# A spectral layer with two MLP layers on one core: weights converted in pairs of 512 columns, and what is done with fetched weights put at other places of a group

## The chip, the cores and the metric

The kernel runs on one core of one Trainium2 chip. The metric is the device time of one execution in microseconds. Five engines work side by side, each through its own instructions in order, and meet at semaphores: PE (TensorE, matmuls), DVE (VectorE), ACT (ScalarE), POOL (GpSimd) and SP (SyncE, which here issues nearly all DMAs). PEld is PE's loading of the stationary operand.

## The reference

Two batches of 3008 rows by 256 columns go through a spectral layer and then, as 6016 tokens, through two MLP layers. Cut to what matters:

```python
def _attn_ref(x, w_r, w_i, b_r, b_i):
    X = np.fft.rfft(x, axis=1)
    ...
    Yr = Xr @ w_r - Xi @ w_i + b_r
    Yi = Xr @ w_i + Xi @ w_r + b_i
    lam = 0.01
    Yr = np.sign(Yr) * np.maximum(np.abs(Yr) - lam, 0.0)
    ...
    y = np.fft.irfft(Y, n=x.shape[1], axis=1)

def _moe_ref(x, w_in, w_out):          # 256 -> 2048 -> 256
    h = x @ w_in
    g = h * (1.0 / (1.0 + np.exp(-1.702 * h)))
    return (g @ w_out).astype(np.float32)
```

The second MLP layer is the same with `np.exp(-h)`. The four weight matrices of the MLP layers arrive as 64-bit floats, bit for bit in integers, and are turned into 32-bit floats on the chip.

## The kernel before

**Stages.** The forward transform (`fwd`, 0 to 78 us), the complex product with threshold (`mid`, to 162), the inverse transform (`inv`, to 223), then the MLP (to about 1275). All matmuls take float32 numbers split into a high part `hi` and a low part `lo` and use three products, hi·hi, hi·lo and lo·hi.

**The MLP.** The tokens stand in six blocks, five of 1024 and a last one of 896. Each block runs through eight groups (p = 0 to 7), a group being 256 of the 2048 hidden columns; a group is written l.i.p here for layer l, block i and p. One group multiplies with seven combinations of the weight's and the input's quarters instead of eight (a scheme like Strassen's): 7 products of 3 matmuls, `prod` (L776), into banks X, Z, Y. ACT copies one product out (L798, L808, L810), DVE adds the next ones to it (L800, L817, L820), ACT applies the activation (L779) and casts its high part (L781), and POOL, for one of the four DVE, subtracts it for the low part (L786). The second matmuls (L748, 24 of them in a group, `out_next`) come a little later from a list. So a group has 21 + 24 = 45 matmuls; `hook(1)` to `hook(6)` are places in a group at which other work is written in. Ahead of each block the 7 combinations of its input are made (`xsums` L686 and L687 in group p = 6, `xprep` in p = 7 and in p = 0 of the new block: ACT casts L696, DVE subtractions L699 and L701).

**The weights.** A matrix is worked on in units of 128 of its 2048 columns or rows (256 numbers on each of 128 partitions), 64 units in all. `cv_load` fetches a raw unit of 256 KB (L146, on SP, two buffers). `cv_bits` converts it: ACT takes the absolute value scaled (L155), five DVE instructions shift and mask the bits (L160 to L164, queued in `fill` and emitted by `pump` or `fills`), and POOL adds the two parts (L223, in `settle`). Weights that are wanted soon are kept, the others spilled to DRAM (L226) and fetched later (L250, `cv_ld`). A first-layer weight, "in", that is kept or fetched gets four sums of its quarters (L195, L196, L198, L200), and the seven slots are cast (L99, ACT) and subtracted (L100) in `place_in`; an "out" weight only needs the cast and the subtraction, in `place_out`.

**What sets the order.** `tf`, `tm` and `ti` list the steps of the three transform stages at which a unit is converted (`tick`). `kb` and `kr` say how many units are converted in a group of block 0, and of blocks 1 to 4: 2 in each group of block 0 and 1 in each group after it. In the last block of layer 0 the weights of layer 1 are fetched, one "in" pair and one "out" pair for a group, and put at hooks 2 and 3 (`moved`). From group 0.0.1 on the program's order is each engine's order. In `fwd` POOL's and SP's order is the program's, in `mid` SP's and in `inv` PE's; there the rest is ordered by a list scheduler on a modelled timeline.

Of the kernel before, what the change touches and what calls it, by code (L numbers as in the profile page):

```python
# [10 lines left out]
CFG = {'lv0': 'V', 'lv': 'VVVVVPVVVVVP', 'dd0': 'VPVVPPPPPVVP', 'dd': 'VVVVVVVVVVPV', 'mpl': 'VPPVVP', 'ths': 'VVVVPV', 'thf': 'PVPVVPVV', 'fsl': 'VPVVVVPV', 'ivf': 'PVVPVVVVVPPVPPVV', 'cva': 'P', 'pol': 'PPPP', 'pil': 'P', 'mvl': 'PVVP', 'xl': 'V', 'xse': 'V', 'gl': 'VPPPPPPP', 'tf': [6, 9, 12], 'tm': [2, 3, 4, 5, 7, 14], 'ti': [2, 2, 3, 4, 5, 10, 12, 13, 13, 15], 'kb': [2, 2, 2, 2, 2, 2, 2, 2], 'kr': 1, 'fa': 3, 'fe': 2, 'xp': [2, 4, 4, 5], 'xq': [1, 4, 1], 'xs': 4, 'xi': [11, 12, 13, 15], 'xsi': 9, 'ca': 4, 'tl': True, 'fwd': 'Pool,SP', 'rest0': 'all', 'rest1': 'all', 'last1': 'all', 'inv': 'PE', 'mid': 'SP', 'last0': 'all', 'thm': 'A', 'gl0': 'PVPVVVPV', 'gl2': 'PPPPPPPP', 'gl3': 'PPPPPPPV', 'xl0': 'V', 'xl1': 'V', 'pre': 17, 'pre2': 0, 'yd': 6, 'nf': 4, 'lvb': 6, 'mlp': 'none', 'pr': 'VVVP', 'pf': 'PV', 'eo': '0000', 'ddb': 6, 'mlp1': 'all', 'mlp2': 'all'}  # L11
# [46 lines left out]
def spectral_mlp_kernel(ctx, tc, xin, m0, mfwd, minv, wc, bias, w_in1, w_out1, w_in2, w_out2, outT):  # L58
# [73 lines left out]
    pairs = [(kind, l, 2 * p, kept) for kind, l, p, kept in WEIGHTS]  # L132
    todo = [(kind, l, c + r, kept) for kind, l, c, kept in pairs for r in range(2)]
    loaded, bits, added, fill = [], [], [], []
    spilled, halves = {}, {}

    def cv_load(k=1):
        for _ in range(min(k, len(todo))):
            kind, l, c, kept = todo.pop(0)
# [33 lines left out]
    def place_out(l, c, a, lo_eng):  # L173
# [888 lines left out]
```

## Time and profile before

| | |
|---|---|
| runs timed | 1282.67, 1284.27, 1284.43 us; median 1284.27 |
| profiled execution | 1280.16 us, its span 1278.4 us |
| mean granted TensorE clock | 0.976 |
| PE busy | 1202.4 us, 94% |
| ACT / DVE / POOL busy | 801.0 / 751.9 / 587.3 us |
| DMA | 57.08 MB, mean 45 GB/s |

The profiled execution is one execution, 4.1 us below the median of the others; times within the trace are against its span. An engine's busy share is an average over stages in which it may be full or nearly idle. In a timeline, "[2.01 <-ACT yt L810]" means that the engine had been idle for 2.01 us and that the instruction of L810 on ACT released it.

### The profile page before, as it was taken

How to read it: one execution, taken by the hardware profiler on the slowest of the kernel's cores; microseconds unless marked ns; L12 is line 12 of the kernel's file. 1: busy time of each engine (PE TensorE's matmuls, PEld its weight loads, DVE VectorE, ACT ScalarE, POOL GpSimd, SP SyncE). 2: the span in 40 equal slices, each digit the busy share in tenths (PEclk: the TensorE clock that was granted, in tenths of full speed). 3: DMA queues.
4: the chain of work that ended last, by engine and by line, in shares of the span. 5: the costliest groups of instructions: out<-in, count | busy, mean ns of one | idle time of the engine just before them, and what ended most of it. 6: DMA issues, size and time to landing. Idle time of an engine off the chain costs nothing.

```text
span 1278.4 us, 15403 instructions
## 1 busy us (share of the span) xinstructions
PE 1202.4 (94%) x5220; PEld 973.4 (76%) x5220; DVE 751.9 (59%) x1222; ACT 801.0 (63%) x1585; POOL 587.3 (46%) x516
## 2 busy tenths in 40 slices
PE   7889869699899999999999879999999999999998
PEld 4867669477688787787887767887888888888897
DVE  7889999777756756657655564243352442623522
ACT  3556544566666667666666667666575665765764
POOL 4667665585444444444443434434333333333343
PEclk9999889989899999999999998999999999999999
DMA  8442114011111111111110110000000000000000
GB/s 321 165 156 62 42 46 154 25 45 46 37 39 37 37 38 34 41 38 33 38 38 9 34 40 27 1 1 34 1 33 1 1 34 1 1 34 1 34 1 29
DMA packets 33009, 57.08 MB, mean 45 GB/s; under 512 B 3233, under 2 KB 22689, under 8 KB 31650
## 3 DMA queue, kind: packets, MB, share of 16 engines
q1 hardware_dynamic: 30882, 41.42, 10.2%
q0 software_dynamic: 2048, 14.68, 3.1%
q8 instruction: 41, 0.67, 0.2%
q14 instruction: 38, 0.31, 0.1%
HBM read 44.68 MB, written 11.40 MB: 44 GB/s over the span
## 4 chain that ended last, share of the span: by engine, by line
PE 55%; ACT 9%; DVE 7%; issue 3%; DVEq 0%; ACTq 0%
PE o L748 29%; PE x L776 26%; ACT yt L779 3%; ACT g L781 2%; DVE yt L817 1%; DVE x L699 1%; ACT yt L798 1%; ACT x L696 1%; DVE yt L800 1%; DVE wi L100 1%; ACT yt L808 0%; DVE cv_c L160 0%; DVE cv_a L162 0%; ACT wi L99 0%; ACT yt L810 0%
## 5 line engine op out<-in xcount | busy, mean ns | idle before, releaser
L786 POOL TENSOR_TENSOR g<-yt,g 128x512 fp32r<-128x512 f32 (+1 forms) x288 | 372.5, 1305 | 567.7 <-DVE g L786 301.2
L748 PE MATMUL o<-g,wo 128*128 128x512 f32 (+1 forms) x2304 | 580.6, 394 | 3.2 <-ACT g L781 1.2
L776 PE MATMUL x<-x,wi 128*128 128x512 f32 (+1 forms) x2016 | 518.6, 396 | 36.6 <-ACT yt L810 15.6
L748 PEld LDWEIGHTS o<-g,wo 128*128 128x128 f32 x2304 | 437.5, 190 | 101.0 <-POOL g L786 1.8
L776 PEld LDWEIGHTS x<-x,wi 128*128 128x128 f32 x2016 | 379.0, 190 | 133.6 <-ACT yt L810 21.7
L779 ACT ACTIVATE yt<-yt 128x512 f32<-128x512 f32 (+1 forms) x288 | 179.0, 622 | 295.2 <-DVE yt L817 248.3
L781 ACT CAST g<-yt 128x512 fp32r<-128x512 f32 (+1 forms) x384 | 234.1, 611 | 11.7
L817 DVE TENSOR_TENSOR yt<-yt,x 128x512 f32<-128x512 f32 (+1 forms) x96 | 64.8, 675 | 210.4 <-PE x L776 210.2
L800 DVE TENSOR_TENSOR yt<-yt,x 128x512 f32<-128x512 f32 (+1 forms) x96 | 64.9, 676 | 174.5 <-ACT yt L798 173.5
L786 DVE TENSOR_TENSOR g<-yt,g 128x512 fp32r<-128x512 f32 (+1 forms) x96 | 66.1, 688 | 66.5 <-ACT g L781 66.4
L699 DVE TENSOR_TENSOR x<-yt,x 128x512 fp32r<-128x512 f32 (+1 forms) x48 | 54.3, 1132 | 28.7 <-ACT x L696 28.7
L223 POOL TENSOR_TENSOR cv_a<-cv_a,cv_c 128x256 f32<-128x256 f32 x64 | 62.9, 988 | 15.7 <-DVE cv_c L164 15.6
L820 DVE TENSOR_TENSOR yt<-yt,x 128x512 f32<-128x512 f32 (+1 forms) x96 | 64.9, 676 | 2.2 <-PE x L776 1.1
L779 ACT ACTIVATE yt<-x 128x512 f32<-128x512 f32 (+1 forms) x96 | 56.2, 585 | 3.9 <-PE x L776 3.9
L810 ACT COPY yt<-x 128x512 f32<-128x512 f32 (+1 forms) x96 | 55.7, 580 | 1.0 <-PE x L776 1.0
L798 ACT COPY yt<-x 128x512 f32<-128x512 f32 (+1 forms) x96 | 54.8, 571 | 1.8 <-PE x L776 1.8
L808 ACT COPY yt<-x 128x512 f32<-128x512 f32 (+1 forms) x96 | 54.9, 571 | 0.0
L358 PE MATMUL psi<-m,fh 128*128 128x376 f32 (+3 forms) x208 | 48.9, 324 | 3.0 <-ACT fh L99 1.7
L498 PE MATMUL psm<-wc_hi,xtl 128*128 128x512 f32 x96 | 40.0, 419 | 4.7 <-DVE xtl L100 3.8
L163 DVE TENSOR_SCALAR cv_c<-cv_a 128x256 uint32<-128x256 uint32 x64 | 43.3, 678 | 1.4
L155 ACT ACTIVATE cv_c<-raw 128x256 f32<-128x256 f32 x64 | 27.4, 438 | 22.9 <-DMA raw<-in_wi 19.8
L358 PE MATMUL psf<-m,xh 128*128 128x376 f32 (+1 forms) x160 | 37.1, 330 | 4.6 <-ACT xh L305 3.6
(109 smaller groups left out, 1140.9 us busy)
## 6 DMA issues: line engine op xcount, KB each, us to landing
raw<-in_wi SPq DMA_DIRECT2D x32, 256.0 KB, 2.7
raw<-in_wo SPq DMA_DIRECT2D x32, 256.0 KB, 2.6
raw<-in_x SPq DMA_DIRECT2D x12, 512.0 KB, 4.8
out_t<-yt SPq DMA_DIRECT2D x20, 256.0 KB, 2.0
m<-in_mf POOLq DMA_DIRECT2D x4, 1128.0 KB, 7.7
m<-in_mi POOLq DMA_DIRECT2D x4, 1128.0 KB, 7.5
w_out<-cv_a SPq DMA_DIRECT2D x24, 128.0 KB, 1.7
cv_ld<-w_out SPq DMA_DIRECT2D x24, 128.0 KB, 2.0
```

The source lines that it names most:

```text
L223: E('cva', u[2]).tensor_add(a, a, c)
L358: nc.tensor.matmul(ps, a, z, start=i == 0 and x == 0, stop=i == last and x == 2)
L699: E('xl1' if l else 'xl0' if i == 0 else 'xl', k).tensor_sub(lo, src, r32(hi))
L748: nc.tensor.matmul(acc[h, mm], st, mv, start=first and k == 0, stop=last and k == 2)
L776: nc.tensor.matmul(ps, st, mv, start=first and m == 0, stop=m == 2, skip_group_check=True)
L779: nc.scalar.activation(g, g if src is None else src, func)
L781: nc.scalar.copy(gh, g)
L786: eng.tensor_sub(gl, g, r32(gh))
L798: nc.scalar.copy(y1, X)
L800: nc.vector.tensor_add(y1, y1, Y)
L817: nc.vector.tensor_add(y2, y2, X)
L820: nc.vector.tensor_add(y3, y3, Z)
```

## The change

A unit becomes a pair: 256 columns or rows, 512 numbers on each partition, 32 pairs. The raw buffer holds a pair (an "in" pair comes by two DMAs, an "out" pair by one) and there is one such buffer in place of two. Each of the conversion's instructions, the POOL addition and the spill is 512 wide and there are half as many. The lists become `tm` [2, 4, 7], `ti` [2, 5, 13] (they were [2, 3, 4, 5, 7, 14] and [2, 2, 3, 4, 5, 10, 12, 13, 13, 15]; `tf` stays [6, 9, 12]), `kb` [1, 1, 1, 1, 1, 1, 1, 0] and `kr` [0, 1, 0, 1, 0, 1, 1, 0]: in the last group of every block and in groups 0, 2 and 4 of blocks 1 to 4 nothing is converted. The core of the rest:

```diff
+            raw = cv_p.tile([P, 2 * CU], mybir.dt.int64, tag="raw", name="raw64", bufs=1)
             if kind == "in":
+                r = raw[:, :].rearrange("p (s f) -> p s f", s=4)
+                src = w[:, 2 * p * P : 2 * (p + 1) * P].rearrange("(k p) f -> p k f", p=P)
+                nc.sync.dma_start(out=r[:, 1:3], in_=src[:, :, :P])
+                nc.sync.dma_start(out=r[:, 0:4:3], in_=src[:, :, P:])
...
-        c = cv_p.tile([P, CU], F32, tag="c", name="cv_c", bufs=4)
-        a = cv_p.tile([P, CU], F32, tag="a", name="cv_a", bufs=N("ca"))
+        c = cv_p.tile([P, 2 * CU], F32, tag="c", name="cv_c", bufs=2)
+        a = cv_p.tile([P, 2 * CU], F32, tag="a", name="cv_a")
...
-        fill.extend(
-            (
-                lambda: add(t12[:, 0], a1[:, 0], a1[:, 1]),
-                lambda: sub(t34[:, 0], a0[:, 0], a1[:, 0]),
-                lambda: put(slice(0, 2), a0),
-                lambda: sub(t12[:, 1], t12[:, 0], a0[:, 0]),
-                lambda: put(2, a1[:, 1]),
-                lambda: sub(t34[:, 1], a0[:, 1], t12[:, 1]),
-                lambda: put(slice(3, 5), t12),
-                lambda: (put(slice(5, 7), t34), w_in.update({(l, p): w})),
-            )
+        return (
+            lambda: add(t[:, 0], a[:, 0], a[:, 3]),
+            lambda: sub(t[:, 2], a[:, 1], a[:, 0]),
+            lambda: sub(t[:, 1], t[:, 0], a[:, 1]),
+            lambda: sub(t[:, 3], a[:, 2], t[:, 1]),
+        ), (
+            lambda: put(slice(0, 3), a[:, 1:4]),
+            lambda: (put(slice(3, 7), t), w_in.update({(l, p): w})),
         )
...
-        fills(1 if l or i == last else 2)
+        fills(1)
...
-    def moved(fetched):
-        for (kind, l, c), tiles in fetched:
-            for r, a in enumerate(tiles):
-                if kind == "in":
-                    place_in(l, c + r, a, nc.vector, sums_c)
-                else:
-                    place_out(l, c + r, a, nc.gpsimd)
+    def moved(h):
+
+        for (kind, l, p), a in fetched:
+            if kind == "in" and h == 2:
+                sums, puts[:] = place_in(l, p, a, nc.gpsimd, sums_c)
+                for f in sums:
+                    f()
+            if kind == "out" and h == 3:
+                place_out(l, p, a, nc.gpsimd)
+        if h == 3:
+            while puts:
+                puts.pop(0)()
...
-                cv_load(2 - len(loaded) if rate(at + 1) else 0)
+                cv_load(1 - len(loaded))
```

So of a fetched "in" weight the four sums are emitted at hook 2, the casts at hook 3, which stands behind the copies L808 and L810, and its low parts move from DVE to POOL. A kept or fetched "in" weight is put with two casts of 384 and 512 columns in place of four. In the whole program DVE has 1032 instructions where it had 1224, ACT 1507 where it had 1587, POOL 473 where it had 521 and SP 133 where it had 189; PE has the same number. Lines behind the conversion stand 3 lines earlier in the changed kernel.

**ACT, a group in the middle of the last block of layer 0** (`wi` and `wo` are the placed weights, `cv_ld` what was fetched, `cv_s` the sums, `g` the high part of an activation, `yt` the token buffer). Before:

```order
L781 CAST g<-yt 128x448
L99 CAST wi_6516<-cv_ld 128x256
L99 CAST wi_6516<-cv_ld 128x128
L99 CAST wi_6516<-cv_s 128x256 x2
L808 COPY yt<-x 128x448
L810 COPY yt<-x 128x448
L99 CAST wo<-cv_ld 128x256 x2
L779 ACTIVATE yt<-yt 128x448
```

And of the changed kernel:

```order
L778 CAST g<-yt 128x448
L805 COPY yt<-x 128x448
L807 COPY yt<-x 128x448
L99 CAST wo<-cv_ld 128x512
L99 CAST wi_6066<-cv_ld 128x384
L99 CAST wi_6066<-cv_s 128x512
L776 ACTIVATE yt<-yt 128x448
```

The two copies stand ahead of every cast of a weight now; before, four casts, two of them of the sums, stood ahead of them.

**DVE, group p = 0 of a new block (1 to 2)** (`x` after `<-` in L817 is a product on PE, `x<-yt,x` in L699 a low part of the block's input). Before:

```order
L800 TENSOR_TENSOR yt<-yt,x 128x512
L699 TENSOR_TENSOR x<-yt,x 128x512 x2
L160 TENSOR_SCALAR cv_c<-cv_c 128x256
L161 TENSOR_SCALAR cv_c<-cv_c 128x256
L162 SCALAR_TENSOR_TENSOR cv_a<-raw_3898,cv_c 128x256
L699 TENSOR_TENSOR x<-tmp,x 128x512
L163 TENSOR_SCALAR cv_c<-cv_a 128x256
L164 SCALAR_TENSOR_TENSOR cv_c<-raw_3898,cv_c 128x256
L752 COPY yt<-o_3428 128x512
L817 TENSOR_TENSOR yt<-yt,x 128x512
```

And of the changed kernel:

```order
L797 TENSOR_TENSOR yt<-yt,x 128x512
L696 TENSOR_TENSOR x<-yt,x 128x512 x2
L696 TENSOR_TENSOR x<-tmp,x 128x512
L749 COPY yt<-o_3156 128x512
L814 TENSOR_TENSOR yt<-yt,x 128x512
```

The five instructions of a conversion that stood between the additions L800 and L817 are gone from this group; so they are in group p = 7 before it.

**SP, at the change from kept to spilled weights, in block 1** (`raw` is the raw buffer, `w_in_0` the place of a spill). Before:

```order
L146 DMA raw_3140<-in_wi 128x2x128
L146 DMA raw_3142<-in_wi 128x2x128
L146 DMA raw_3258<-in_wi 128x2x128
L146 DMA raw_3260<-in_wi 128x2x128
L226 DMA w_in_0_3277<-cv_a 128x256
L226 DMA w_in_1_3280<-cv_a 128x256
L146 DMA raw_3367<-in_wi 128x2x128
L226 DMA w_in_2_3386<-cv_a 128x256
L146 DMA raw_3460<-in_wi 128x2x128
```

And of the changed kernel:

```order
L145 DMA raw_2911<-in_wi 128x2x128
L146 DMA raw_2911<-in_wi 128x2x128
L145 DMA raw_3188<-in_wi 128x2x128
L146 DMA raw_3188<-in_wi 128x2x128
L223 DMA w_in_0_3206<-cv_a 128x512
L145 DMA raw_3350<-in_wi 128x2x128
L146 DMA raw_3350<-in_wi 128x2x128
L223 DMA w_in_1_3368<-cv_a 128x512
```

Each raw tile is now written by two DMAs, into the one buffer that the conversion before it has read, and the spills are half as many and twice as large.

## Rows read from the trace of the kernel before

**Rows 1.** The windows view: from and to (us) and length, then busy time of PE, PEld, DVE, ACT and POOL with their instructions, the granted clock, the DMA share and GB/s. The row is `mid` and `inv` together.

```profile
78.00:223.00 145.00, 130.52 (x612) 107.77 (x612) 143.38 (x242) 79.12 (x155) 94.27 (x84) 0.93 0.24 81
```

**Rows 2.** Groups of DVE's instructions by line and shape in 78 to 223 us: busy time, mean ns of one, idle time before them. They are the conversion.

```profile
L164 DVE SCALAR_TENSOR_TENSOR cv_c<-raw,cv_c 128x256 f32<-128x256 uint32 x15 | 9.9, 668 | 0.0
L162 DVE SCALAR_TENSOR_TENSOR cv_a<-raw,cv_c 128x256 uint32<-128x256 uint32 x15 | 9.8, 661 | 0.0
...
L161 DVE TENSOR_SCALAR cv_c<-cv_c 128x256 uint32<-128x256 uint32 x15 | 7.8, 525 | 0.1
L160 DVE TENSOR_SCALAR cv_c<-cv_c 128x256 f32<-128x256 f32 x15 | 7.4, 502 | 0.5 <-ACT cv_c L155 0.5
L163 DVE TENSOR_SCALAR cv_c<-cv_a 128x256 uint32<-128x256 uint32 x15 | 6.5, 436 | 0.0
```

**Rows 3.** The same view of DVE in the forward transform, 0 to 78 us: two lines of the conversion, and L336, a tensor_scalar 512 wide.

```profile
L164 DVE SCALAR_TENSOR_TENSOR cv_c<-raw,cv_c 128x256 f32<-128x256 uint32 x5 | 2.1, 412 | 0.0
...
L161 DVE TENSOR_SCALAR cv_c<-cv_c 128x256 uint32<-128x256 uint32 x5 | 1.3, 277 | 0.0
...
L336 DVE TENSOR_SCALAR wc_lo<-wc_lo 128x512 fp32r<-128x512 f32 x1 | 0.4, 407 | 0.0
```

**Rows 4.** The same view of POOL, first in 78 to 223 us, then of the whole span.

```profile
L223 POOL TENSOR_TENSOR cv_a<-cv_a,cv_c 128x256 f32<-128x256 f32 x15 | 18.9, 1262 | 15.6 <-DVE cv_c L164 15.6
...
L786 POOL TENSOR_TENSOR g<-yt,g 128x512 fp32r<-128x512 f32 x240 | 316.4, 1330 | 487.2 <-DVE g L786 296.4 <-PE x L776 67.8 <-DVE yt L752 48.0
```

**Rows 5.** PE's timeline (start, duration, operation, how many in a row, wait ahead): the first row of 12 output matmuls in groups of block 0 and at its end, and after them the waits view of 223 to 350 us (total, times, longest).

```profile
255.04 6.03 PE L748 MATMUL o<-g,wo 128*128 128x512 f32 x12 [1.17 <-ACT g L781]
...
319.95 2.96 PE L748 MATMUL o<-g,wo 128*128 128x512 f32 x12
...
348.41 2.96 PE L748 MATMUL o<-g,wo 128*128 128x512 f32 x12
...
PE x L776 <- DVE yt L817: 10.5, 6, 3.4
```

**Rows 6.** PE's timeline at the border of blocks 1 and 2 of layer 0, and (last two rows) in layer 1 from group p = 7 of block 0 to the start of block 2, nine groups.

```profile
411.41 2.96 PE L748 MATMUL o<-g,wo 128*128 128x512 f32 x12
...
429.44 2.33 PE L776 MATMUL x<-x,wi 128*128 128x512 f32 x9 [1.17 <-DVE yt L817]
...
434.77 2.96 PE L748 MATMUL o<-g,wo 128*128 128x512 f32 x12
...
861.29 2.96 PE L748 MATMUL o<-g,wo 128*128 128x512 f32 x12
...
956.63 2.96 PE L748 MATMUL o<-g,wo 128*128 128x512 f32 x12
```

**Rows 7.** PE's timeline in the last block of layer 0 and, last two rows, of layer 1; the sixth row is the waits view of 692 to 800 us.

```profile
695.89 1.50 PE L776 MATMUL x<-x,wi 128*128 128x448 f32 x6 [2.01 <-ACT yt L810]
...
702.77 2.62 PE L748 MATMUL o<-g,wo 128*128 128x448 f32 x12
...
757.11 2.63 PE L748 MATMUL o<-g,wo 128*128 128x448 f32 x12
...
763.35 2.61 PE L776 MATMUL x<-x,wi 128*128 128x448 f32 x6 [3.61 <-ACT yt L810]
...
787.79 2.96 PE L748 MATMUL o<-g,wo 128*128 128x512 f32 x12
...
PE x L776 <- ACT yt L810: 15.6, 8, 3.6
...
1208.40 2.63 PE L748 MATMUL o<-g,wo 128*128 128x448 f32 x12
...
1217.64 2.63 PE L748 MATMUL o<-g,wo 128*128 128x448 f32 x12
```

**Rows 8.** The timeline of all engines inside group 0.5.3 of that block.

```profile
714.24 1.23 DVE L100 TENSOR_TENSOR wi<-cv_ld,wi 128x256 fp32r<-128x256 f32 x1 [0.91 <-ACT wi L99]
715.39 0.28 DVE L198 TENSOR_TENSOR cv_s<-cv_s,cv_ld 128x128 f32<-128x128 f32 x1
...
715.70 0.81 ACT L99 CAST wi<-cv_s 128x256 fp32r<-128x256 f32 x2 [1.30 <-DVE cv_s L198]
...
717.43 1.50 PE L776 MATMUL x<-x,wi 128*128 128x448 f32 x6 [1.27 <-ACT yt L810]
```

**Rows 9.** The timelines of DVE and (third row) POOL in group p = 6 of a block in which both `xsums` and a conversion stand, and of DVE in an ordinary group.

```profile
485.40 0.69 DVE L800 TENSOR_TENSOR yt<-yt,x 128x512 f32<-128x512 f32 x1 [2.06 <-ACT yt L798]
...
488.04 1.38 DVE L160 TENSOR_SCALAR cv_c<-cv_c 128x256 f32<-128x256 f32 x1
...
487.55 1.73 POOL L786 TENSOR_TENSOR g<-yt,g 128x512 fp32r<-128x512 f32 x1
...
491.04 0.69 DVE L817 TENSOR_TENSOR yt<-yt,x 128x512 f32<-128x512 f32 x1
...
459.54 0.69 DVE L817 TENSOR_TENSOR yt<-yt,x 128x512 f32<-128x512 f32 x1 [1.50 <-PE x L776]
```

**Rows 10.** DMA issues of the page (KB each, us to landing), and the waits view of ACT over the span.

```profile
raw<-in_wi SPq DMA_DIRECT2D x32, 256.0 KB, 2.7
...
raw<-in_x SPq DMA_DIRECT2D x12, 512.0 KB, 4.8
...
ACT cv_c L155 <- DMA raw<-in_wi: 19.8, 7, 5.2
```

More of the change, by code (lines that the diff above doesn't have):

```diff
@@ L234, in window @@
             if u[0] == "in":
-                place_in(u[1], u[2], a, E('pil', u[2]), sums_tmp)
+                for part in place_in(u[1], u[2], a, E('pil', u[2]), sums_tmp):
+                    fill.extend(part)
             else:
@@ L244, in tick, with fetch @@
         pump()
-        cv_load(2 - len(loaded))
-    def fetch(kind, l, c):
-        tag, n = ("a", 4) if kind == "in" else ("ld", 2)
-        a = cv_p.tile([P, CU], F32, tag=tag, name="cv_ld", bufs=n)
-        nc.sync.dma_start(out=a, in_=spilled[kind, l, c])
+        cv_load(1 - len(loaded))
+    def fetch(kind, l, p):
+        a = cv_p.tile([P, 2 * CU], F32, tag="a" if kind == "in" else "ld", name="cv_ld", bufs=2 if kind == "in" else 1)
+        nc.sync.dma_start(out=a, in_=spilled[kind, l, p])
         return a
@@ L837, in spectral_mlp_kernel @@
     for c in range(0, NFC // 2, 2):
-        moves.setdefault((0, 0, c // 2), []).append(("out", 0, c))
+        moves.setdefault((0, 0, c // 2), []).append(("out", 0, c // 2))
     for p in range(NPR):
-        moves.setdefault((0, last, p + 1) if p < NPR - 1 else (1, 0, 0), []).append(("in", 1, 2 * p))
-        moves.setdefault((0, last, p + 3) if p < NPR - 3 else (1, 0, p - NPR + 3), []).append(("out", 1, 2 * p))
-    def moved(fetched):
-        for (kind, l, c), tiles in fetched:
-            for r, a in enumerate(tiles):
-                if kind == "in":
-                    place_in(l, c + r, a, nc.vector, sums_c)
-                else:
-                    place_out(l, c + r, a, nc.gpsimd)
+        moves.setdefault((0, last, p + 1) if p < NPR - 1 else (1, 0, 0), []).append(("in", 1, p))
+        moves.setdefault((0, last, p + 3) if p < NPR - 3 else (1, 0, p - NPR + 3), []).append(("out", 1, p))
+    def moved(h):
[9 more added lines that the diff above has]
+                puts.pop(0)()
+    puts = []
     def rate(at):
@@ L854, in rate @@
         l, i, p = seq[at]
-        return 0 if l == 1 or i == last else N('kb')[p] if i == 0 else N('kr')
+        return 0 if l == 1 or i == last else N('kb' if i == 0 else 'kr')[p]
     def fetch_for(at):
-        units = moves.get(seq[at], ()) if at < len(seq) else ()
-        return [(u, [fetch(u[0], u[1], u[2] + r) for r in range(2)]) for u in units]
+        return [(u, fetch(*u)) for u in (moves.get(seq[at], ()) if at < len(seq) else ())]
     fetched = fetch_for(0)
@@ L886, in hook @@
                 xsums(*nxt)
-            if h == (3 if len(done) < 3 else 1):
+            if h == (3 if len(done) < 2 else 1):
                 window(0, done)
@@ L892, in hook @@
             if h in (2, 3):
-                moved([f for f in fetched if (f[0][0] == "in") == (h == 2)])
+                moved(h)
             if h == 5:
```

44 lines of the change are left out of this document (19 added, 25 removed).

## The prediction

> **What bounds the kernel now.** I read the windows view first, to see which engine is full in which stage; then PE's timeline, to see where the spacing of equal groups differs; then the waits of those places, and the timeline of all engines inside one such group.
>
> Three kinds of place come out. Ahead of the MLP, in `mid` and `inv`, DVE is busy for 143.38 of 145 us, while PE works for 130.52 [rows 1]: what DVE does there sets the pace. In most of the MLP PE is full: in layer 1 nine groups from 861.29 to 956.63 take 95.34 us, 10.5 each and 0.84 over [rows 6]. There nothing but fewer matmuls would help, and the change leaves PE's instructions alone. Between these lie the places with a spacing above 10.5 us (9.24 for 448 columns, 1217.64 − 1208.40 [rows 7]): block 0, the borders of blocks in layer 0, and its last block. There PE waits for an addition on DVE (L817) or a copy on ACT (L810), because those stand in order behind weight conversion or weight placing. So the question is how much of this excess goes, place by place.
>
> **The change part by part.** The sum is made against the profiled execution, 1280.16 us, and then set against the median of the runs, 1284.27.
>
> *Conversion ahead of the MLP.* 15 units are converted in 78 to 223 us and cost DVE 9.9 + 9.8 + 7.8 + 7.4 + 6.5 = 41.4 us, 2.76 each [rows 2]. Undisturbed, in the forward transform, the two kinds take 412 and 277 ns [rows 3], so a unit is 2 × 0.41 + 3 × 0.28 = 1.66; the other 1.10 is what POOL beside it and the crowd cost. A pair of 512 columns undisturbed is 3 × 0.41 (L336, [rows 3]) + 2 × 0.69 (the 512-wide L817, [rows 9]) = 2.6. If the disturbance stays 1.10 for a chain of five instructions, a pair costs 3.7, and 7.5 pairs cost 28: 14 us saved. If it doubles with the width, 4.8 and 36: 5 us saved. Part of what DVE saves will not reach the end, since PE has only 14.5 us of idle time in this stretch [rows 1]. Against it stands one raw buffer in place of two: a pair can be fetched only when L164 of the pair before has read it. ACT already waits 19.8 us in seven waits for raw units of 256 KB that land 2.7 us after issue; 512 KB of `in_x` took 4.8 [rows 10]. The list spreads pairs over steps of about 7 us, so most of this is covered by the transforms' other work; if two pairs in `inv`, where ACT also does the copies, were caught in full, it would cost 2 × 4.8 − 5 ≈ 4. I take 7, between −4 and 14, nearer the dear pair because POOL's additions get wider too (L223 alone has a mean of 1.26 us at 256 columns, [rows 4]).
>
> *Conversion in block 0.* From 255.04 to 319.95 five groups take 64.91 us, 12.4 over 52.5; six waits for L817 make 10.5 us of waiting in the block [rows 5]. Two units a group, ten DVE instructions, become one pair, five instructions: 3.3 undisturbed becomes 2.6, and where POOL's wide subtractions alternate with them, five places for it instead of ten. That is 0.7 to 2 us for each of seven groups, in 4 or 5 of which the wait ends last. I take 5. The bound above is 10 (nearly all of the waits); below, −1: `fills(1)` now puts the whole chain at one place, and wide instructions hold L817 up for longer when it is ready in their midst.
>
> *The border of blocks 0 and 1.* Two groups from 319.95 to 348.41 take 28.46, 7.5 over 21 [rows 5]. Layer 1 has the same border without conversion, at 0.84 over [rows 6]. As groups p = 7 and p = 0 have no conversion now, up to 6.6 goes. What is late next is the input's combinations (L699), whose chain is as long in both layers; after a stall the first matmuls also ran slowly: 12 in 6.03 us at 255.04 where 2.96 is usual [rows 5, 6], TensorE's lower clock. I take 5.5 (3 to 6.6).
>
> *The borders 1 to 2, 2 to 3 and 3 to 4.* The first takes 434.77 − 411.41 = 23.36 us for two groups, 2.36 over, 1.17 of it waiting for L817 [rows 6]; the same in layer 1 is inside the stretch that has only 0.84 over in nine. Three borders are 7.1. But group p = 6 of blocks 1 to 4 keeps a conversion beside `xsums`. There L800 ends at 486.1, the sums and a 256-wide chain follow, and L817 starts at 491.04 without having waited for PE: no slack at all, with L160 drawn out to 1.38 us beside a POOL subtraction of 1.73 [rows 9]. A 512-wide chain is 2.6 − 1.66 = 0.9 longer, so PE waits some 0.8 in four such groups, 3.2. In an ordinary group L817 still waits 1.50 for PE [rows 9], which covers the 0.9. Net 4 (2 to 6).
>
> *The last block of layer 0, its middle.* In a group the casts of the sums (ACT, 715.70) wait 1.30 us for L198, which stands behind L100, itself drawn out to 1.23 us; the copies L808 and L810 come behind those casts, and PE waits 1.27 us for L810 [rows 8]. Five groups from 702.77 to 757.11 take 54.34, 8.1 over 46.2, and the group before waits 2.01 at 695.89 [rows 7]. With the casts behind both copies, ACT has nothing in front of them that waits for a sum. The sums stay on DVE, without the low parts: fewer instructions ahead of L817. What is late next is POOL: it gets low parts of 384, 512 and 512 columns, at 1.33 for 512 [rows 4] about 3.7 us, between its subtractions of `g`. Its three subtractions of `g` take at most 3 × 1.33 = 4.0, together 7.7 of a group's 9.24, so I expect them to fit, if tightly. I take all of it, 10 (8 to 10.1).
>
> *Its last group and the first of layer 1.* From 757.11 to 787.79 two groups take 30.68; 9.24 + 10.5, and half a us because products are already 512 wide, leave 10.5 over, with a wait of 3.6 at 763.35 [rows 7]. Here `xprep` and the placing meet in one group; the placing still has to be done (the first group of layer 1 wants its weight), so I take 7 (4 to 10).
>
> Fewer DMAs on SP and 80 fewer instructions on ACT I cost at nothing: PE's work in the MLP hides both; uncovered, ACT's 48 casts saved would be at most a gain inside the last two terms.
>
> The sum: 7 + 5 + 5.5 + 4 + 10 + 7 = 38.5. That makes 1241.7 of the profiled execution, and 1245.8 of the median, for which I say 1246.
>
> **The rivals.**
>
> *A. POOL and DVE hold each other up as long as before.* L160 took 1.38 us beside a POOL instruction that took 1.73, where 0.28 and 1.33 are usual [rows 3, 4, 9]; so both are stretched by overlap, and a wider instruction may simply be stretched for longer. Against it: a chain has half as many places at which this can happen. Then the first two terms are nothing and the stall of group 6 doubles (four times 1.6 leave 0.7 of that term): 5.5 + 0.7 + 10 + 7 = 23, 1261 us. The Trainium skill, "SBUF — State Buffer", section "Who interferes with whom", says this outright: a DVE instruction with two SBUF inputs contends with GpSimd's reads, and whoever holds the shared port pair in DVE's two-port modes keeps it for the whole instruction while the other stands still. The stretched rows agree; that the loss grows with the width no row here shows. By that rule the sum would be 23, without it 38.5.
>
> *B. The stall moves to POOL.* Low parts of fetched weights now queue ahead of those of `g`, and output matmuls wait for them. For it: three of a group's four low parts of `g` are POOL's, and a low part of 512 takes as long as one of `g` [rows 4]; against it, the 1.5 us that are left of a group. If 1 us in each of the eight groups comes back, 8.5 of the last two terms' 17 go: 1254.
>
> *C. The clock comes along.* In 78 to 223 us the granted clock is 0.93 [rows 1], so 0.07 × 145 = 10 us hang on it. If a steadier stream there lets TensorE stay at the upper of its levels, up to that is added: 1236.
>
> *D, slower: the single raw buffer.* A fetch starts only after the pair before has been read, ACT's L155 waits for it, and ACT's copies and casts for PE queue behind L155. If all nine pairs ahead of the MLP pay 4.8 us [rows 10] on the path, that is 43 in place of a gain of 7; with the other 31.5 the change loses 11.5: 1296. It decides from 31.5 / 9 = 3.5 us a pair. Against it: DVE, not the fetch, ended nearly everything there, and the ticks lie far apart.
>
> *E. It comes to nothing.* A and B together with a small loss ahead of the MLP: 1284.
>
> The Trainium skill, "Perfetto Trace Analysis", section "Optimizing Scalar/DVE Operations", says that larger instructions help where the engine is saturated, and that smaller ones may finish a needed result sooner where it isn't but causes bubbles elsewhere. Rows 1 put `mid` and `inv` in the first case; rows 9 put group 6 in the second. By the second half, group 6 gets worse, as in my fourth term; by the first alone that term would be 7.1 and the sum 41.6.
>
> **How the numbers follow.** The forecast 0.52, A 0.17, B 0.10, C 0.13, D 0.05, E 0.03. The likeliest one's own range, from the bounds of its terms taken together, is 1236 to 1256. To hold eight in ten it has to reach A above and C below: 1229 to 1265. A measurement of this kernel can tell about 0.2%, 2.6 us, from no change. A, B, C and the forecast are all faster by more: 0.92. Within that: E, 0.03. Slower: D, 0.05.
>
> **What would show it.** In the profile of the changed kernel: groups of the last block at 9.24 us and no wait for the second copy (L807 there); the border of blocks 0 and 1 at 22 to 24 us for two groups instead of 28.46, later borders at 21; a wait of about 0.8 for L814 in group 6 of blocks 1 to 4; the five lines of a pair at 3.7 to 4.8 us ahead of the MLP, and the start of the MLP some 7 us earlier than 223. A shows as POOL's and DVE's 512-wide means far above 1.33 and 0.69 and an unmoved start; B as waits of output matmuls for POOL in the last block; D as long waits of L155 for `raw`. I am wrong if the start of the MLP moves back, or if most of the excess of the last block is still there.

## The result and the profile after

Three runs of the changed kernel took 1249.27, 1249.22 and 1248.68 us, median 1249.22, against 1284.27 before: a ratio of 0.9729, 95% interval 0.9707 to 0.9752. The forecast was 1246, so 35.05 us of the 38.5 came. The profiled execution took 1249.27 us, with a span of 1247.4; against the profiled execution of before that is 31.0 us, and the other 4.1 are what that one execution lay below its own median.

From the page of the changed kernel, its engines (busy, share, instructions) and one line of its groups:

```profile
PE 1190.4 (95%) x5220; PEld 967.2 (78%) x5220; DVE 708.4 (57%) x1030; ACT 790.1 (63%) x1505; POOL 593.3 (48%) x468
...
L773 PE MATMUL x<-x,wi 128*128 128x512 f32 (+1 forms) x2016 | 513.5, 393 | 20.9 <-ACT yt L807 8.6
```

PE's idle time ahead of its product matmuls fell from 36.6 us to 20.9, and its busy time by 12.0 us for the same 5220 matmuls; where that comes from follows with the table below. POOL is busier by 6 us with fewer instructions: they are wider, and it has the low parts that DVE gave up.

The windows view of the stretch ahead of the MLP, which answers to [rows 1], and DVE's lines in it, which answer to [rows 2]; L534 is work that has nothing to do with the weights:

```profile
78.00:221.00 143.00, 130.12 (x609) 107.78 (x609) 137.97 (x201) 74.80 (x136) 87.18 (x71) 0.93 0.24 81
...
L534 DVE TENSOR_TENSOR f<-th 128x256 f32<-128x256 f32 x28 | 22.8, 857 | 0.2
...
L165 DVE SCALAR_TENSOR_TENSOR cv_a<-raw,cv_c 128x512 uint32<-128x512 uint32 x7 | 7.2, 1025 | 0.0
L167 DVE SCALAR_TENSOR_TENSOR cv_c<-raw,cv_c 128x512 f32<-128x512 uint32 x7 | 6.8, 965 | 0.1
...
L166 DVE TENSOR_SCALAR cv_c<-cv_a 128x512 uint32<-128x512 uint32 x7 | 4.8, 682 | 0.0
L164 DVE TENSOR_SCALAR cv_c<-cv_c 128x512 uint32<-128x512 uint32 x7 | 4.7, 677 | 0.1
...
L163 DVE TENSOR_SCALAR cv_c<-cv_c 128x512 f32<-128x512 f32 x7 | 2.9, 414 | 0.1
```

The chain is now 7.2 + 6.8 + 4.8 + 4.7 + 2.9 = 26.4 us for seven pairs, 3.77 each, where 15 units took 41.4. DVE's busy time fell by 5.4 us only, in a stretch 2 us shorter. In the same view of before L534's line reads:

```profile
L537 DVE TENSOR_TENSOR f<-th 128x256 f32<-128x256 f32 x28 | 16.1, 619 | 0.1
```

These 28 subtractions and additions, the same in both kernels, take 6.7 us more.

PE's timeline from the MLP's start on, first matmuls of a product and the rows of 12 output matmuls that answer to [rows 5 to 7]:

```profile
221.39 2.95 PE L773 MATMUL x<-x,wi 128*128 128x512 f32 x12
...
246.18 2.93 PE L773 MATMUL x<-x,wi 128*128 128x512 f32 x6 [6.09 <-ACT yt L807]
...
266.06 2.96 PE L745 MATMUL o<-g,wo 128*128 128x512 f32 x12
...
316.59 2.96 PE L745 MATMUL o<-g,wo 128*128 128x512 f32 x12
...
337.63 2.97 PE L745 MATMUL o<-g,wo 128*128 128x512 f32 x12
...
676.59 2.63 PE L745 MATMUL o<-g,wo 128*128 128x448 f32 x12
685.83 2.63 PE L745 MATMUL o<-g,wo 128*128 128x448 f32 x12
...
732.25 2.63 PE L745 MATMUL o<-g,wo 128*128 128x448 f32 x12
...
756.86 2.96 PE L745 MATMUL o<-g,wo 128*128 128x512 f32 x12
```

Each of these stands at the same place of the program as a row of before: 316.59 as 319.95, 337.63 as 348.41, 685.83 as 702.77, 732.25 as 757.11, 756.86 as 787.79; 676.59 as 691.26, 266.06 as 268.66 and 221.39 as 223.13, three more rows of before's timeline. The lengths between them give the account:

| stretch | before | after | gained | forecast |
|---|---|---|---|---|
| up to the MLP's start | 223.13 | 221.39 | 1.7 | 7 |
| block 0, to its last group | 96.82 | 95.20 | 1.6 | 5 |
| border of blocks 0 and 1 | 28.46 | 21.04 | 7.4 | 5.5 |
| from there to the last block, with three borders and the group ahead of the fourth | 342.85 | 338.96 | 3.9 | 4 |
| last block, six groups | 65.85 | 55.66 | 10.2 | 10 |
| its last group and the first of layer 1 | 30.68 | 24.61 | 6.1 | 7 |
| all | | | 30.9 | 38.5 |

The last four came as forecast within 2 us, the first two at a third and less. In block 0, 6.09 us of waiting in one group stay, for a copy on ACT, and 5.9 in four waits for L814; the kernel before waited 8.8 us there in four waits for L817, and never for L810.

Part of two lines of the table is the clock. The windows view of the border of blocks 0 and 1 and of the last line's two groups, before and then after:

```profile
319.95:348.41 28.46, 24.96 (x91) 18.62 (x90) 20.94 (x35) 18.05 (x36) 13.05 (x14) 0.88 0.13 37
757.11:787.79 30.68, 23.94 (x91) 19.87 (x90) 18.46 (x34) 22.19 (x45) 10.81 (x11) 0.83 0.09 26
```

```profile
316.59:337.63 21.04, 21.04 (x91) 16.81 (x90) 14.22 (x19) 15.95 (x31) 10.38 (x8) 1.00 0.00 1
732.25:756.86 24.61, 21.16 (x92) 16.42 (x91) 18.42 (x27) 20.21 (x38) 16.29 (x13) 1.00 0.11 33
```

With the stalls gone TensorE was granted its upper level all the way, 1.00 where the mean was 0.88 and 0.83, and PE was busy for 3.9 and 2.8 us less with the same matmuls. So 3.9 of the 7.4 us and 2.8 of the 6.1 are faster matmuls, the rest shorter waits.

### The profile page after: what moved, and what is told of

Read it like the earlier page. It is cut to its first block, busy times and chain, and to the rows that moved or that the text cites. A ratio compares the mean times of both kernels' runs of the same rounds, so it can differ in the third digit from the quotient of the medians.

```text
span 1247.4 us, 14957 instructions
## 1 busy us (share of the span) xinstructions
PE 1190.4 (95%) x5220; PEld 967.2 (78%) x5220; DVE 708.4 (57%) x1030; ACT 790.1 (63%) x1505; POOL 593.3 (48%) x468
## 4 chain that ended last, share of the span: by engine, by line
PE 68%; DVE 15%; ACT 8%; issue 5%; POOL 3%; DMA 1%; SPq 0%; DVEq 0%; POOLq 0%; ACTq 0%
PE o L745 35%; PE x L773 31%; ACT yt L776 2%; ACT g L778 2%; DVE f L534 1%; PE psf L352 1%; DVE fl L100 1%; DVE cv_a L165 1%; DVE cv_c L166 1%; DVE th L518 1%; DVE yt L665 1%; DVE cv_c L163 1%; ACT x L693 1%; DVE yt L797 1%; DVE yt L814 1%
## 5 line engine op out<-in xcount | busy, mean ns | idle before, releaser
L783 POOL TENSOR_TENSOR g<-yt,g 128x512 fp32r<-128x512 f32 (+1 forms) x288 | 377.2, 1322 | 535.7 <-DVE g L783 275.2
L745 PE MATMUL o<-g,wo 128*128 128x512 f32 (+1 forms) x2304 | 574.3, 391 | 1.8 <-POOL g L783 1.2
L773 PE MATMUL x<-x,wi 128*128 128x512 f32 (+1 forms) x2016 | 513.5, 393 | 20.9 <-ACT yt L807 8.6
L745 PEld LDWEIGHTS o<-g,wo 128*128 128x128 f32 x2304 | 433.1, 188 | 97.6 <-POOL g L783 2.3
L814 DVE TENSOR_TENSOR yt<-yt,x 128x512 f32<-128x512 f32 (+1 forms) x96 | 64.8, 675 | 230.6 <-PE x L773 230.5
L817 DVE TENSOR_TENSOR yt<-yt,x 128x512 f32<-128x512 f32 (+1 forms) x96 | 64.8, 675 | 0.7
L696 DVE TENSOR_TENSOR x<-yt,x 128x512 fp32r<-128x512 f32 (+1 forms) x48 | 49.8, 1038 | 25.6 <-ACT x L693 25.6
L795 ACT COPY yt<-x 128x512 f32<-128x512 f32 (+1 forms) x96 | 54.8, 571 | 5.3 <-PE x L773 3.7
L220 POOL TENSOR_TENSOR cv_a<-cv_a,cv_c 128x512 f32<-128x512 f32 x32 | 48.7, 1523 | 12.9 <-DVE cv_c L167 12.2
L495 PE MATMUL psm<-wc_hi,xth 128*128 128x512 f32 x96 | 40.5, 422 | 4.4 <-ACT xth L99 4.4
L355 PEld LDWEIGHTS psi<-m,fh 128*128 128x128 f32 x208 | 38.1, 201 | 6.6 <-DVE sd L508 4.6
L495 PE MATMUL psm<-wc_hi,xtl 128*128 128x512 f32 x96 | 38.5, 406 | 1.6 <-DVE xtl L100 1.6
L355 PE MATMUL psi<-m,fl 128*128 128x376 f32 (+3 forms) x104 | 34.8, 334 | 5.4 <-DVE fl L100 3.0
```

The source lines that it names most:

```text
L355: nc.tensor.matmul(ps, a, z, start=i == 0 and x == 0, stop=i == last and x == 2)
L495: nc.tensor.matmul(t, a, w, start=(n == 0), stop=(n == 11 and grp == 1))
L745: nc.tensor.matmul(acc[h, mm], st, mv, start=first and k == 0, stop=last and k == 2)
L773: nc.tensor.matmul(ps, st, mv, start=first and m == 0, stop=m == 2, skip_group_check=True)
L783: eng.tensor_sub(gl, g, r32(gh))
L814: nc.vector.tensor_add(y2, y2, X)
```

## The experiments

All start from the changed kernel unless it is said otherwise; the ratios are against the kernel before on the same chip. Where an edit adds lines, lines behind it stand 2 to 5 later.

**The kernel before once more.**

> The kernel before as it is, for a second profile: the first one's execution was 4.1 us below the median. If a stage varies between executions, the MLP's start (223.1 us there) moves by some us in this one, while the groups from 0.1.2 on keep their lengths to 0.05 us; if nothing varies, 1280 us and 223 again.

1283.62 us. The first matmul of the MLP in it, by PE's timeline:

```profile
225.73 1.55 PE L776 MATMUL x<-x,wi 128*128 128x512 f32 x6
```

That is 2.6 us later than in the first profile, while from group 0.1.2 to the middle of the last block each group is as long as there to 0.05 us. So the stretch ahead of the MLP varies from execution to execution. The changed kernel and eight of the kernels below have the same work in the same order ahead of the MLP on PE, DVE, ACT and POOL; theirs starts at 219.4 to 222.4, 220.7 in the mean. Against 224.4, the mean of before's two, the first line of the table is rather 3.7 than 1.7. Much of the spread is made in the forward transform: the first product of `mid` stands at 76.4 to 79.1 us, and from there to the MLP's start the nine take 143.0 to 144.3, before's two 144.9 and 147.4.

**The chain in halves.**

```diff
-                lambda: ts(c, c, C_HI, None, op0=ALU.min),
+        for h in range(2):
+            v = slice(h * CU, (h + 1) * CU)
...
+                    lambda v=v: ts(c[:, v], c[:, v], C_HI, None, op0=ALU.min),
...
```

> Each of the five DVE instructions of a pair's conversion is split into two of 256 columns; all else is the changed kernel (loads, buffers, tables, places). Theory (what a pair costs on DVE is per instruction, disturbance by POOL included): a pair ahead of the MLP costs 2 x 2.76 = 5.5 us instead of 3.77, seven pairs 12 us more of DVE time, of which the MLP's start shows a part (2 to 6 us later than 221.4) and block 0 another 2 to 4; 1252 to 1258 us. Rival (the width of the instructions is nothing, the gain came from where things stand): within 2 us of 1249.

1263.62 us (four runs, 1262.67 to 1265.19; ratio 0.9847, 0.9832 to 0.9862). More than the theory's range: of the 14.4 us the MLP's start has 5.6 (227.0), the groups to 0.1.1 five, nearly all of them in the group behind the placing of two in-weights (a wait of 3.03 us for the addition L816), and group 6 with its border some 0.85 in each of four blocks. Two lines of DVE ahead of the MLP:

```profile
L165 DVE TENSOR_SCALAR cv_c<-cv_c 128x256 f32<-128x256 f32 x14 | 9.4, 707 | 0.4 <-ACT cv_c L158 0.4
...
L169 DVE SCALAR_TENSOR_TENSOR cv_c<-raw,cv_c 128x256 f32<-128x256 uint32 x14 | 5.5, 409 | 0.0
```

The five lines (L165 to L169 here) are 33.2 us for seven pairs, 4.74 each instead of 3.77: 6.8 us more of DVE time, nearly all of it seen at the start. The width of the five instructions, with the order that the list scheduler makes of it, is thus worth 14 us, 40% of the change. The MLP also starts later here than in either execution of before, with less chain time (33.2 against 41.4): something else in the changed stretch costs some us. Which it is (one raw buffer, fewer and larger ticks, the other order of the list scheduler) was not tried apart and stays open.

**Three of five instructions left out ahead of the MLP.**

```diff
+        if pre:
+            del fill[-2]
+            del fill[-4:-2]
```

> Of the conversions ahead of the MLP three of the five DVE instructions are left out (L163, L164, L166, so these weights are wrong), about 12 us of DVE time between 78 and 221 us. Theory (DVE is still what paces that stretch): the MLP starts 7 to 12 us earlier, at 209 to 214. Rival (after the change something else ends there, waits between mid and the inverse transform or the clock): it starts at 216 or later, though DVE is less busy.

One run, 1246.08 us. The rival holds:

```profile
78.00:221.00 143.00, 131.59 (x624) 108.45 (x624) 133.25 (x187) 77.85 (x145) 81.76 (x67) 0.96 0.23 78
...
217.78 2.49 PE L778 MATMUL x<-x,wi 128*128 128x512 f32 x10
```

Of the chain L165 and L167 are left, 10.6 us, and 2.4 of one pair that still has all five, together 13.0 instead of 26.4; but DVE's busy time falls from 137.97 to 133.25 only, and the MLP starts 2.9 us ahead of the mean of 220.7. Counted from the first product of `mid`, 139.2 us against 143.0 to 144.3, it is some 4. So 13.4 us of instructions gone are worth 3 to 4 at the start, and DVE's busy share, 93% even here, is not a measure of what it holds up. Two of its waits in this kernel:

```profile
DVE th L523 <- ACT sd L518: 3.1, 3, 1.5
...
DVE sd L512 <- PE psm L500: 1.9, 2, 1.7
```

DVE now waits for ACT and for PE in turn. Beside the halves, where 6.8 us more cost 5.6, this points to a knee: the changed kernel would stand about where shorter chains stop to pay. These are two single executions in a stretch that varies by up to 3 us, so the size of the knee isn't shown.

**The additions ahead of the MLP on DVE.**

```diff
-            E('cva', u[2]).tensor_add(a, a, c)
+            (nc.vector if pre else E('cva', u[2])).tensor_add(a, a, c)
```

> The additions L220 of the pairs converted ahead of the MLP are DVE's and not POOL's; all else is the changed kernel. Theory (ahead of the MLP the time saved in the chain is partly eaten by DVE's other instructions, which stretch beside POOL's): with 11 us of POOL's wide additions gone, DVE's other instructions from the first product of mid to the MLP's start take 4 to 7 us less than their 126.8, about as much as seven additions add (5 us), and the MLP starts where it did, 219 to 222. Rival (the stretching has nothing to do with POOL): the others stay at 126 to 128 and the start moves back to 222 to 225.

One run, 1247.04 us, MLP from 218.73, 2.0 ahead of the mean and just under the theory's 219 to 222. The 2.0 are made in the forward transform, which ends at 73.6 us here; from there to the MLP's start it is 145.2, longer than in any of the nine.

What POOL does to DVE can be read from the traces one instruction at a time. In the changed kernel's, the same instruction of the chain in two pairs, with POOL idle and beside a subtraction on POOL:

```profile
158.11 0.41 DVE L166 TENSOR_SCALAR cv_c<-cv_a 128x512 uint32<-128x512 uint32 x1
...
169.94 1.48 POOL L540 TENSOR_TENSOR fd<-f,fb 128x512 f32<-128x512 f32 x1
170.18 1.52 DVE L166 TENSOR_SCALAR cv_c<-cv_a 128x512 uint32<-128x512 uint32 x1
```

So it is throughout: of DVE's 327 instructions up to the MLP's start the 156 that ran beside no POOL instruction are all within 0.04 us of the shortest of their kind (same operation, tiles and shape, in any of the traces). What the others take above that shortest is the disturbance. The 28 of L534 have 409 to 414 ns where they ran alone, eight times, and 1036 in the mean beside POOL, twenty times; before it was twelve and sixteen. The 24 that read a matmul's result where PE left it, in PSUM (L507 and L508, `sd<-us,psm`), take 0.68 us either way. DVE's instructions from the execution's start to the MLP's, added up for six executions (us), each as what they would take at their shortest plus the disturbance; the conversion has the eight additions in the last line:

| | conversion and sums | DVE's other work | disturbance in all | MLP's start |
|---|---|---|---|---|
| before | 36.9 + 24.4 | 137.2 + 31.9 | 56.3 | 223.1 |
| before once more | 36.9 + 28.1 | 137.2 + 32.4 | 60.5 | 225.7 |
| changed | 30.0 + 11.2 | 137.2 + 46.2 | 57.4 | 221.4 |
| chain in halves | 36.9 + 18.3 | 137.2 + 36.4 | 54.7 | 227.0 |
| three of five left out | 19.0 + 8.4 | 137.2 + 47.1 | 55.5 | 217.8 |
| additions on DVE | 35.4 + 11.3 | 137.2 + 38.1 | 49.4 | 218.7 |

The change took 20 us out of the conversion, 13 of them disturbance, and DVE's other work, which it left as it was, got 14 longer. In the eight further executions of the same program ahead of the MLP the disturbance in all is 54.8 to 58.0. So it hardly depends on how long or how wide the chain is: what the chain loses the other work gains. It fell with POOL's additions gone, to 49.4; 8 of the 14 us come back in the other work, 3.5 of them behind the first product of `mid`, a little under the 4 to 7 of the theory, and the eight additions cost DVE 9.1.

**Pairs at the borders again.**

```diff
-'kb': [1, 1, 1, 1, 1, 1, 1, 0], 'kr': [0, 1, 0, 1, 0, 1, 1, 0]
+'kb': [1, 1, 1, 1, 1, 1, 1, 1], 'kr': [1, 0, 1, 0, 1, 0, 0, 1]
```

> Only the two tables differ: a pair is converted in p = 7 of block 0 too, and in p = 0, 2, 4 and 7 of blocks 1 to 4 (instead of 1, 3, 5, 6). Theory (a conversion at the border holds up the new block's input): the border of blocks 0 and 1 costs 4 to 8 us more and the borders after it 1.5 to 3 each, while group 6 loses its 0.9 us stall in four blocks; 1256 to 1266 us. Rival (half as many, wider instructions would have mended the border by themselves): under 1252 us.

1270.64 us (four runs, 1270.43 to 1271.72; ratio 0.99, 0.9884 to 0.9917), 21.4 more, beyond the theory's range. PE's timeline at the border of blocks 1 and 2:

```profile
410.36 2.96 PE L745 MATMUL o<-g,wo 128*128 128x512 f32 x12
...
417.40 2.38 PE L773 MATMUL x<-x,wi 128*128 128x512 f32 x9 [1.28 <-DVE yt L814]
...
431.00 3.78 PE L773 MATMUL x<-x,wi 128*128 128x512 f32 x9 [2.63 <-DVE yt L814]
...
437.43 2.96 PE L745 MATMUL o<-g,wo 128*128 128x512 f32 x12
```

It waits 1.28 and 2.63 for the addition behind the chain, and the two groups take 27.07 us, where the kernel before with its 256-wide units waited 1.17 and took 23.36 [rows 6]. So at a border a pair in each of two groups is worse than a unit in each was (it is also twice as many columns); that the border got better is the tables' doing, and with this one the change would be worth 13 us instead of 35.

**None in group 6.**

```diff
-'kr': [0, 1, 0, 1, 0, 1, 1, 0]
+'kr': [0, 1, 1, 1, 0, 1, 0, 0]
```

> Only the table of blocks 1 to 4 differs: a pair is converted in groups 1, 2, 3, 5 instead of 1, 3, 5, 6, so none stands beside the new block's two sums in group 6. Theory (sums and a 512-wide chain overrun the additions there): the excess of about 0.9 us round group 6 goes in four blocks, 3.3 us less in all, 1245.5 to 1246.5 us. Rival (two pairs in neighbouring groups 1, 2, 3 wait for the one raw buffer and stall there instead): 1249 or more.

1246.18 us (four runs, 1244.71 to 1247.35; ratio 0.9709, 0.9695 to 0.9724), 3.0 less than the changed kernel; the two intervals overlap, but the trace shows where the time went. No group from 0.1.2 to 0.4.6 is over 10.5 us, and no three pairs in a row stall. The 0.8 us of my fourth term was right: in the changed kernel the two groups round the sums of group 6 had 0.4 and 0.5 over, in each of blocks 1 to 3.

**What made the last block: four arrangements of one placing.** Here a fetched in-weight's four sums (DVE), two casts (ACT) and two low parts are put at other places. First the casts, and with them the low parts on POOL, ahead of the copies, as before, and all sums first:

```diff
                 for f in sums:
                     f()
+                while puts:
+                    puts.pop(0)()
```

> The two casts of a fetched in-weight and its low parts stand at hook 2 again, right behind the sums and ahead of the copies L805 and L807; the low parts stay on POOL, the instructions stay wide, the out-weight stays at hook 3. Theory (the order of casts and copies on ACT made the 9.9 us in the middle of the last block): groups of the last block of layer 0 go from 9.24 back to 10.2 to 10.8 and the last block costs 8 to 16 us more, 1257 to 1265 us. Rival (fewer and wider instructions, or the low parts' move to POOL, made it): groups stay within 0.3 of 9.24, under 1252 us.

1259.23 us (four runs, 1256.65 to 1261.14; ratio 0.981, 0.9795 to 0.9826). The time lies in the range of the theory, the place doesn't: the groups 0.5.2 to 0.5.5 stay at 9.24. What it costs comes in the last two and the first of layer 1:

```profile
PE x L773 <- ACT yt L807: 10.3, 3, 4.2
```

So my theory of the middle of the block fell. Two more tell it apart, this one with DVE's low parts back as well (`place_in(l, p, a, nc.vector, sums_c)`):

> As e2_hook2 (casts of a fetched in-weight at hook 2, ahead of the copies), and its low parts on DVE again, behind the four sums. It tells what made the 1.55 us a group in the middle of the last block. If the low parts on DVE made it (they stand between the sums and the addition L814, and slow each other with POOL), those groups take 10.2 to 10.8 us again; if it was that sums stood behind low parts, so that the casts of the sums came late, they stay at 9.24 to 9.4, since all four sums come first here.

One run, 1255.87 us; the middle stays at 9.24, so the low parts' move to POOL is not it either:

```profile
695.39 2.63 PE L745 MATMUL o<-g,wo 128*128 128x448 f32 x12
704.63 2.63 PE L745 MATMUL o<-g,wo 128*128 128x448 f32 x12
```

And with sums and low parts mixed as before:

```diff
+                sums, late = place_in(l, p, a, nc.vector, sums_c)
+                for f in (*sums[:2], late[0], *sums[2:], late[1]):
+                    f()
```

> As e9_lo_dve, with the order inside hook 2 of the kernel before: two sums, the cast and low part of the first slots, the other two sums, the cast and low part of the other slots; instructions stay wide. If the place of the sums behind a low part is the cause, groups in the middle of the last block take 10.2 to 10.8 us here and 9.24 to 9.4 in e9_lo_dve; if it is the number of instructions (four casts and four low parts before, two and two here), 9.24 to 9.4 in both.

One run, 1266.27 us; the groups take 11.05 us, 1.8 over and more than expected. PE's rows of two, and the timeline of one, which with wide instructions reads as [rows 8] did:

```profile
696.82 2.63 PE L745 MATMUL o<-g,wo 128*128 128x448 f32 x12
707.87 2.63 PE L745 MATMUL o<-g,wo 128*128 128x448 f32 x12
```

```profile
697.63 1.27 DVE L100 TENSOR_TENSOR wi<-cv_ld,wi 128x384 fp32r<-128x384 f32 x1 [1.04 <-ACT wi L99]
...
699.46 0.62 ACT L99 CAST wi<-cv_s 128x512 fp32r<-128x512 f32 x1 [1.86 <-DVE cv_s L198]
...
700.40 0.54 ACT L807 COPY yt<-x 128x448 f32<-128x448 f32 x1
...
700.99 1.29 PE L773 MATMUL x<-x,wi 128*128 128x448 f32 x5 [1.54 <-ACT yt L807]
```

DVE's low part waits for ACT's first cast, the sums wait behind it, ACT's second cast waits for the sums, the copy behind that, and PE for the copy: DVE and ACT wait for each other twice in a row. Last, the same mixture behind the copies:

> As e10_mixed (sums and low parts of a fetched in-weight mixed on DVE as before, instructions wide), but the whole at hook 3, behind the copies L805 and L807. It tells whether casts behind the copies would have been enough by themselves in the middle of the last block. If they are, groups 0.5.2 to 0.5.5 take 9.24 to 9.4 us here as they do with early sums alone (e9_lo_dve); if the mixed sums and low parts then hold up the addition L814 instead, 9.8 to 11.

One run, 1266.31 us; groups of 11.23, 2.0 over and above the range again, and the wait has changed its name:

```profile
PE x L773 <- DVE yt L814: 4.3, 5, 1.7
```

So casts behind the copies would not have been enough in the middle: the mixed row then stands ahead of the addition L814. Sums ahead of low parts are what mended it. Casts behind the copies are worth the other part, at the block's end. There the sums themselves come late, behind the next block's input; in e2_hook2, where the casts stand ahead:

```profile
737.47 0.62 ACT L99 CAST wi<-cv_s 128x512 fp32r<-128x512 f32 x1 [3.49 <-DVE cv_s L198]
...
739.01 2.61 PE L773 MATMUL x<-x,wi 128*128 128x448 f32 x6 [4.22 <-ACT yt L807]
```

**A faster one.** The wait of 6.09 us in block 0 is of the same kind. POOL, DVE and ACT of the changed kernel there:

```profile
241.39 1.28 POOL L100 TENSOR_TENSOR wi<-tmp,wi 128x512 fp32r<-128x512 f32 x1
...
242.71 1.07 DVE L195 TENSOR_TENSOR tmp<-cv_a 128x128 f32<-128x128 f32 x1 [0.87 <-POOL wi L100]
...
244.53 0.62 ACT L99 CAST wi<-tmp 128x512 fp32r<-128x512 f32 x1 [3.42 <-DVE tmp L198]
...
245.54 0.59 ACT L807 COPY yt<-x 128x512 f32<-128x512 f32 x1
```

The second weight's sums wait until POOL has read `tmp` for the first one, ACT's cast waits 3.42 us for them, and the copies stand behind the cast.

```diff
+                sums, late = place_in(u[1], u[2], a, E('pil', u[2]), sums_c if n else sums_tmp)
+                fill.extend(sums)
+                (puts if n else fill).extend(late)
```

> An attempt at a faster one: the table of e5_no6, and of two kept in-weights that are placed in one group (0.0.1) the second has its sums in a c buffer, not in the one tmp that POOL's low part of the first still reads, and its casts behind the copies. PE waited 6.09 us there for L807. If the casts of the second on ACT were what held the copies up, 2 to 4 us of that go: 1242 to 1244. If the wait only moves to POOL's queue or to the chain ahead of L814, 1245 to 1247.

1241.82 us (four runs, 1239.75 to 1242.79; ratio 0.9685, 0.9669 to 0.9701): 7.4 less than the changed kernel and 4.4 less than with the table alone. That wait is gone, and 1.91 and 1.49 close behind it have come for it. Whether the other buffer or the later casts did it was not tried apart.

**And one that isn't.**

```diff
+        fill.extend(ops[:3])
+        tail.extend(ops[3:])
...
+        while k is None and tail:
+            tail.pop(0)()
```

> A further attempt at a faster one: b1_no6_late, and of each chain of five DVE instructions in the MLP the last two stand at hook 4, behind the additions L814 and L817 and the subtraction L783, where DVE waited some 2 us. Theory (the 512-wide chain ahead of L814 is what is left over in groups 0.0.3 to 0.0.6, some 1.5 to 2.3 us each): 4 to 6 us less, 1236 to 1238. If the later end of the chain holds up the fetch into the one raw buffer, so that L158 waits and the copies behind it: 1241 or more.

1251.50 us (four runs, 1250.18 to 1251.97; ratio 0.9755, 0.9737 to 0.9773), 9.7 more than without it. ACT's and PE's timelines in group 0.0.4:

```profile
278.35 0.67 ACT L159 ACTIVATE cv_c<-raw 128x512 f32<-128x512 f32 x1 [2.45 <-DMA raw<-in_wi]
```

```profile
281.22 1.67 PE L778 MATMUL x<-x,wi 128*128 128x512 f32 x6 [1.44 <-ACT yt L812]
```

The chain's last instruction reads the raw buffer later, the fetch into it starts later, ACT waits for the fetch, and the copies behind wait with it: from the MLP's start to 660 us ACT waits 36.0 us for raw weights in 13 waits, and 1.0 in one without the edit. This is rival D of the prediction, at another place.

## Why the prediction was right, and where not

The direction, the time and four of six places came as worked out. The time came nearer than the terms did: against the profile that they were read from 30.9 of the 38.5 us came, 8.7 short in the first two terms and 1.1 over in the others. That the runs are only 3.5 off is luck in part, since the execution profiled before lay 4.1 under its median. By the prediction's own steps:

*Ahead of the MLP (7 forecast, 1.7 by the profiles, some 3.7 over executions).* The price of a pair was right, 3.77 against 3.7 to 4.8: 2.6 undisturbed and 1.17 of disturbance, where a unit had 1.10. The step that failed is that DVE keeps what the chain saves, and with it "what DVE does there sets the pace". Of the 20 us that left the conversion 14 are spent again as disturbance of DVE's other work, and leaving out 13.4 us more of its instructions brought 3 to 4. PE did end `mid` earlier in the profiles, at 156.7 instead of 162.2; then the inverse transform waits longer for the last of `mid` on DVE (first row after, second before):

```profile
PE psi L355 <- DVE sd L508: 4.2, 2, 2.8
```

```profile
PE psi L358 <- DVE sd L511: 1.3, 2, 0.8
```

*Block 0 (5 forecast, 1.6).* The step that failed is "0.7 to 2 us for each of seven groups". The four groups from 266.06 to 316.59 take 50.5 us, against 51.3 from 268.66 to 319.95 before, and 50.0 with the chain in halves: there the width is worth nothing. Its 5 us lie ahead of them, where the chain meets the placing (from the MLP's start 44.7 us, in halves 50.1), and there the change brought a wait for a copy that the kernel before didn't have, 6.09 us (where that had 3.41 for L817) for two in-weights placed in one group through one `tmp`, with their casts ahead of the copies: I had costed the chain there and not the placing. It was not among the rivals. Of the 10.5 us of waits that I put to block 0, 1.7 lie at the border.

*The border of blocks 0 and 1 (5.5 forecast, 7.4)* and *the later borders (4 forecast, 3.9)* came for the reason given; e4_border and e5_no6 bear out both signs of the latter, the gain at the border and the loss in group 6. That the clock would come along at the first border I had named only as what slows PE after a stall; it is 3.9 of the 7.4 us.

*The last block (10 forecast, 10.2).* The size was right, since the whole excess went, but the reason only in part. That the casts wait for sums which stand behind a low part was read rightly from [rows 8]; that it is the casts' place behind the copies which mends it was wrong for the middle. The early sums do it, and either order of casts and copies is then as good. POOL's low parts fit, as estimated.

*The last group and the first of layer 1 (7 forecast, 6.1).* Here the casts' place is the cause: with it put back, e2_hook2 loses 10 us, more than the whole gain. The clock makes 2.8 of it.

Of the rivals, A's mechanism is borne out ahead of the MLP: POOL and DVE held each other up as long as before, 57.4 us of disturbance against 56.3 and 60.5. By the terms the change lies midway between A's sum (23) and the forecast's (38.5), at 30.9: the first two terms came to 3.4, not to nothing, the stall of group 6 did not double, and the first border gave more. The Trainium skill's rule on the ports that DVE and GpSimd share, that a DVE instruction with two SBUF inputs contends with GpSimd's reads ("SBUF — State Buffer", section "Who interferes with whom"), agrees: L534 has two such inputs and takes longer beside POOL alone. That the loss grows with the width, as I took it for A, the halves don't bear out for the chain, since a pair in halves costs more (4.74 us) than a whole one (3.77). B did not show: PE waited for no low part in the last block. C did not come ahead of the MLP, where the granted clock stayed at 0.93; it came at the border of blocks 0 and 1 and at the end of the last block. D cost next to nothing ahead of the MLP: ACT's L158 waited 1.0 us for raw weights there, in two waits, where L155 had waited 17.6. It cost the 9.7 us of b5_split.

## What to carry to other kernels

When two engines hand pieces back and forth (sum, cast, low part, sum, cast), emit everything that one of them can do without the other first; the place of the pieces in the other engine's row matters only where the first engine is late anyway. Wider instructions pay where an engine has no gaps, and cost where a short result is waited for, so a change of width has to come with a new look at which groups get the work. A busy share near 100% on an engine whose instructions another engine draws out is no proof that it is the bound: leave some of its work out and see what the end does. And the disturbance doesn't belong to the instructions that show it: with a shorter or wider chain as much of it fell on others here, and only less work on POOL made it smaller.

## What was not expected

The same program ahead of the MLP started it at 219.4 to 222.4 us in nine kernels, while groups in the middle of the MLP repeat to 0.05 us. The clock goes with it: up to the MLP's start the granted clock is 0.95 in the earliest of them and 0.92 in the latest; which of the two moves the other no run here shows. A difference of 2 us there can't be read from one profile, even where the total repeats to 0.1%.

An instruction's duration in the trace can contain what another engine does to it: the same 28 operations of 128x256 on DVE had a mean of 619 ns before and of 857 after, no wait of that length is listed for them, and those that ran beside no POOL instruction took 0.41 us in both.
